# At most two loads to a place, and a conversion load only where there is no other: the order of SP's transfers in an attention and feed-forward kernel

## The chip, the cores and the metric

The kernel runs on one core of a Trainium2 chip. The metric is the device time of one execution in microseconds. The profile shows one execution, with its own times counted from the start of its span.

## The reference

Attention with its heads mixed before and after the softmax, then a feed-forward layer with the gate h - tanh(h). Batch 8, 12 heads, 448 rows, head dimension 64; 3584 tokens of 768, inner dimension 2048.

```python
scores = scale * np.matmul(q, k.transpose(0, 1, 3, 2))
scores = np.einsum('bhij,hg->bgij', scores, w_pre)
attn = softmax(scores)                      # over the last axis
attn = np.einsum('bhij,hg->bgij', attn, w_post)
x = np.matmul(attn, v)                      # then heads side by side: 3584 x 768
h = x @ w_in
out = (h - np.tanh(h)) @ w_out
```

In the kernel, `w_in` and `w_out` arrive as 64-bit numbers; they are turned on the chip into pairs of 32-bit parts (high and low) and written back to DRAM, from where the feed-forward stage reads them.

## The kernel before, in words

**Places.** Attention is cut into 32 blocks (8 batches of 4 runs of up to 120 rows), and these into 360 groups of rows. The main loop (L832) goes through places p = 0 to 182; places up to 179 take two groups each. A place issues, in this order: the gathers of the groups two places ahead (L507, tile `t` from the scores `s`), up to six waiting transfers (`issue`, L372), the mix of heads before the softmax (`premix`, L513, into `ps_p`), the normalizer of the place before (`norm`, L536: DVE's `zs`, POOL's `wr` at L543), the softmax (`expo`, L524: DVE's maxima at L530, ACT's exponentials at L532), then scores, preparation of q and k, and values by a table of places, then the mix after the softmax of the place before (`mix`, L548: PE at L560 into `ps_o`). The copy of `ps_o` to `at` on ACT (L570, L577) is issued at the start of the next place.

**The queues.** All these gathers and transfers are issued by SP, in the order of the program. Loads of q, k and v and stores of the result x go to a Python list `queue`; those of the conversion of weights go to a second list, `slow`. `issue(6)` sends up to six entries at each place: first from `queue`, then from `slow`, each list in its own order, and only what was asked for in an earlier place. `now` (L635) sends all that waits.

**The conversion.** `narrow_steps` (L38) goes through 56 chunks of the weights. Up to three chunks are loaded or at work, up to two at work. A chunk is taken up when its load was sent in an earlier place (`landed(1)`). `narrow_chunk` (L71) does one in eleven steps: DVE L80, ACT L82 with DVE L83, ACT L85, DVE L87, DVE L89, DVE L94, POOL L96, POOL L98, ACT L102, POOL L104, and the request of two stores. Tiles: `cr` the load, `cm`, `cs`, `cl` buffers, two of each; `ws` the place in DRAM. `Steps.place` (L861, in every place from 4 on) runs steps at a fixed rate, 617 steps over 164 places; a step taken while no chunk is at work does nothing. At place 177 `conv.rest(now)` (L867) runs all that is left, sending each transfer at once.

**The end of attention.** After that, still in place 177, SP issues the first weight tile (`w`, L334) and twelve loads of x (`rx`, L238). Place 178 casts the first x on ACT (`xh`, L246), place 180 the other five, and place 181 runs the first hidden matmuls of the feed-forward stage (L257 to L262).

Of the kernel before, what the change touches and what calls it, by code (L numbers as in the profile page):

```python
# [18 lines left out]
DRAM = bass.MemoryType.DRAM  # L19
# [129 lines left out]
def kernel_body(  # L149
# [189 lines left out]
    with ExitStack() as st:  # L339
# [20 lines left out]
        queue, slow, sent = [], [], {}  # L360
# [6 lines left out]
        def send(x, engine):  # L367
            entry = x.pop(0)
            engine.dma_start(*entry[1:3])
            entry[3] = place[0]  # L370

        def issue(most):  # L372
            for x in (queue, slow):
                while x and most and x[0][0] < place[0]:
                    send(x, nc.sync)
                    most -= 1

# [306 lines left out]
        for w in range(2):  # L684
            for at in AT[w]:
                x = repeat[:, w, at : at + HP].rearrange("p (i h) -> p i h", i=GH)
# [7 lines left out]
        for w in range(2):  # L694
            for a in range(2):
                if w == 0:
                    x = both[:, w, a].rearrange("p (i g) -> p i g", i=GH)
                    of, step = ps_w[:, w, :].unsqueeze(1).to_broadcast([P, GH, H]), [[H, GH], [0, H]]
                else:
                    x = both[:, w, a].rearrange("p (g i) -> p g i", i=GH)  # L700
# [68 lines left out]
        while halved:  # L769
            ready = sorted((x for x in halved if x[0] <= p), key=lambda x: (x[1], x[3:]))  # L770
            if ready:
                x = ready[0]
# [3 lines left out]
                if x[2] == kind and other and x[1] > p + 1:  # L776
                    x = other[0]
# [54 lines left out]
        for p in range(NPL + 3):  # L832
# [4 lines left out]
            for t in (2 * p + 4, 2 * p + 5):  # L837
                if t < NG:
                    gather(t)
            issue(6)  # L840
            if p == NPL + 1:
                for f in start.pop(p):
# [105 lines left out]
```

## Time and profile before

| | |
|---|---|
| median of 3 runs | 1788.36 us |
| lowest and highest | 1786.55 and 1803.96 us |
| the profiled execution's own time | 1788.92 us |
| its span | 1787.2 us |
| mean granted clock of TensorE | 0.993 |
| transfers issued by SP: gathers `t` | 342 of 210 KB, 16 of 189 KB |
| loads of the conversion `cr` | 24 of 512 KB, 32 of 384 KB |
| stores of the conversion `ws` | 48 of 256 KB, 64 of 192 KB |
| loads of v, k, q | 24 and 23 of 448 KB, 23 of 360 KB and 8 of 264 KB |

Attention lasts until about 845 us of the span; there the first hidden matmul starts. In the rows of a timeline, the first number is the start in us, the second the length, then engine, line, operation, tiles and count; in brackets stands how long the engine had been idle and what released it. `SPq` is the queue of SP, and its rows are the issues of transfers, not the transfers.

### The profile page before, as it was taken

Reading aid. Unit: us, or ns where it says so; the run is one execution under the profiler, and the core shown is the slowest. Engines: PE = TensorE matmul, PEld = TensorE weight load, DVE = VectorE, ACT = ScalarE, POOL = GpSimd, SP = SyncE. Lnnn points to the kernel's source line nnn. Section 1 sums busy time; section 2 is a strip of 40 time slices with the busy share of each in tenths; the row PEclk is TensorE's granted clock in tenths of the full one; section 3 lists DMA queues with packets and bytes.
Section 4 is the critical chain, followed back from the end, with each engine's and each line's share of the span. In section 5 each row is a group of like instructions: output and inputs, shape, how many; then the busy total and the mean of one; then the engine's idle time right before and its main releaser. Section 6 shows DMA issues by size and latency. Waiting matters only on the chain.

```text
span 1787.2 us, 41382 instructions
## 1 busy us (share of the span) xinstructions
PE 1751.0 (98%) x16572; PEld 1425.6 (80%) x16572; DVE 1128.3 (63%) x2362; ACT 1000.5 (56%) x2051; POOL 320.1 (18%) x417
## 2 busy tenths in 40 slices
PE   8999999999999999999999999999999999999998
PEld 6777777777777777777888888888888888888887
DVE  5676777777777767664556566565565565655555
ACT  5777877777777776765343443433434434444333
POOL 1333333333333333321010010000000000000000
PEclk9999999999999999999999999999999999999999
DMA  8668687777967687565655655655656655655651
GB/s 176 204 196 216 194 236 224 217 215 215 249 203 218 215 213 220 178 202 216 255 207 194 248 193 207 241 193 214 229 197 216 224 208 204 228 217 190 230 194 36
DMA packets 232816, 372.32 MB, mean 208 GB/s; under 512 B 98992, under 2 KB 207536, under 8 KB 218288
## 3 DMA queue, kind: packets, MB, share of 16 engines
q1 hardware_dynamic: 231740, 368.45, 64.0%
q8 instruction: 131, 2.15, 0.5%
q10 hardware_dynamic: 884, 1.22, 0.2%
q14 instruction: 61, 0.50, 0.1%
HBM read 245.37 MB, written 47.19 MB: 164 GB/s over the span
## 4 chain that ended last, share of the span: by engine, by line
PE 87%; DMA 4%; ACT 4%; DVE 3%; issue 1%; POOL 0%; SPq 0%; ACTq 0%; DVEq 0%; POOLq 0%
PE ps_o L560 13%; PE ps_h L257 8%; PE ps_h L258 8%; PE ps_h L262 8%; PE ps_m L602 8%; PE ps_p L521 7%; PE ya L305 6%; PE ya L302 6%; PE ya L303 6%; PE ps_q L477 5%; PE yb L305 3%; PE yb L303 3%; PE yb L302 3%; DMA t<-s 2%; PE ps_m L443 1%
## 5 line engine op out<-in xcount | busy, mean ns | idle before, releaser
L560 PEld LDWEIGHTS ps_o<-wr,e 60*112 60x112 f32 (+1 forms) x5760 | 306.2, 176 | 44.3 <-POOL wr L543 21.8
L560 PE MATMUL ps_o<-wr,e 60*112 60x60 f32 (+1 forms) x5760 | 315.5, 259 | 14.3 <-POOL wr L543 7.7
L530 DVE TENSOR_REDUCE mx<-ps_p 128x1 f32<-128x448 f32 x360 | 207.7, 619 | 163.9 <-PE ps_p L521 163.7
L532 ACT ACTIVATE e<-ps_p,mx 128x448 f32<-128x448 f32 x360 | 225.7, 634 | 101.9 <-DVE mx L530 99.4
L289 ACT CAST gh<-r 128x512 fp32r<-128x512 f32 x112 | 69.6, 621 | 372.6 <-DVE r L282 372.6
L258 PE MATMUL ps_h<-xl,w 128*128 128x512 f32 x672 | 264.4, 393 | 0.0
L257 PE MATMUL ps_h<-xh,w 128*128 128x512 f32 x672 | 264.3, 393 | 0.0
L570 ACT COPY at<-ps_o 112x960 f32<-112x960 f32 x156 | 153.7, 985 | 93.8 <-PE ps_o L560 93.2
L247 POOL TENSOR_TENSOR xl<-rx,xh 128x512 fp32r<-128x512 f32 x38 | 55.6, 1464 | 731.2 <-ACT xh L246 731.2
L521 PE MATMUL ps_p<-t,wpre 60*64 60x448 f32 (+1 forms) x1440 | 180.8, 569 | 3.9 <-DMA t<-s 2.7
L305 PE MATMUL ya<-w,gl 128*128 128x512 f32 x448 | 177.0, 395 | 0.7 <-DVE gl L290 0.7
L278 DVE SCALAR_TENSOR_TENSOR r<-qa,ps_h 128x512 f32<-128x512 f32 x112 | 77.1, 688 | 159.2 <-ACT t L275 159.2
L302 PE MATMUL ya<-w,gh 128*128 128x512 f32 x448 | 174.8, 390 | 1.0 <-ACT gh L289 1.0
L303 PE MATMUL ya<-w,gh 128*128 128x512 f32 x448 | 174.8, 390 | 0.0
L602 PEld LDWEIGHTS ps_m<-at,vr 112*64 112x64 f32 x3072 | 147.5, 137 | 31.0 <-ACT at L577 10.9
L262 PE MATMUL ps_h<-xh,w 128*128 128x512 f32 x672 | 170.6, 389 | 0.0
L602 PE MATMUL ps_m<-at,vr 112*64 112x120 f32 (+1 forms) x3072 | 161.6, 261 | 8.4 <-ACT at L577 3.1
L272 ACT ACTIVATE u<-ps_h 128x512 f32<-128x512 f32 x112 | 67.0, 599 | 152.9 <-PE ps_h L262 152.9
L262 PEld LDWEIGHTS ps_h<-xh,w 128*128 128x128 f32 x672 | 126.3, 188 | 26.3
L258 PEld LDWEIGHTS ps_h<-xl,w 128*128 128x128 f32 x672 | 127.5, 190 | 23.7
L257 PEld LDWEIGHTS ps_h<-xh,w 128*128 128x128 f32 x672 | 127.4, 190 | 23.4
L543 POOL TENSOR_TENSOR wr<-wpost,zs 128x120 f32<-128x120 f32 x180 | 70.2, 390 | 402.9 <-DVE zs L542 293.6
(93 smaller groups left out, 3038.0 us busy)
## 6 DMA issues: line engine op xcount, KB each, us to landing
w<-ws SPq DMA_DIRECT2D x112, 1536.0 KB
t<-s SPq DMA_DIRECT2D x342, 210.0 KB
cr<-in_moe_w_in_dram SPq DMA_DIRECT2D x24, 512.0 KB
cr<-in_moe_w_out_dram SPq DMA_DIRECT2D x32, 384.0 KB
vr<-in_v_dram SPq DMA_DIRECT2D x24, 448.0 KB
kr<-in_k_dram SPq DMA_DIRECT2D x23, 448.0 KB
out_dram<-ob SPq DMA_DIRECT2D x24, 384.0 KB
qr<-in_q_dram SPq DMA_DIRECT2D x23, 360.0 KB
```

What stands on the lines that cost most here:

```text
L257: nc.tensor.matmul(ph, wh[:, fs], xh, start=(c == 0), stop=False)
L258: nc.tensor.matmul(ph, wh[:, fs], xl, start=False, stop=False)
L262: nc.tensor.matmul(ph, wl[:, fs], xh, start=False, stop=(c == NK - 1))
L302: nc.tensor.matmul(y, gh[:, tok], wh[:, es], start=first, stop=False)
L303: nc.tensor.matmul(y, gh[:, tok], wl[:, es], start=False, stop=False)
L305: nc.tensor.matmul(y, gl[:, tok], wh[:, es], start=False, stop=last)
L521: nc.tensor.matmul(pss[r][halves[j], :], wpre[k, :], ts[j][k, :], start=True, stop=True)
L530: nc.vector.tensor_reduce(out=mx, in_=ps, axis=AX.X, op=ALU.max, negate=True)
L532: nc.scalar.activation(e, ps, AF.Exp, bias=mx, scale=1.0, accum_out=zs[:, 0, r : r + 1])
L560: nc.tensor.matmul(ps[:CP, j, c * GP : (c + 1) * GP].rearrange("p (h i) -> p h i", i=GI)[:, :, r * GH : (r + 1) * GH], e[k, c * CP : (c + ...
L570: nc.scalar.copy(ats[i0][:, :, :, at : at + 2 * GI].rearrange("p c h (j i) -> p j (c h) i", j=2), ps[:CP, :, : NC * GP].rearrange("p j (x ...
L602: nc.tensor.matmul(pv[j * D : (j + 1) * D, r, :n], vt[:, j, c, :], ats[i][:, c, 2 * hp + j, :n], start=(c == 0), stop=(c == NC - 1),)
```

## The change

`issue` counts the loads that it sends at a place (entries whose target is not in DRAM). It stops with a list when two loads have gone, and stops with `slow` at a load if any load has gone at that place. Stores are not counted, but one that stands behind a held load in its list waits with it.

```diff
         def issue(most):
+
+            loads = 0
             for x in (queue, slow):
                 while x and most and x[0][0] < place[0]:
+                    if x[0][1].space != DRAM:
+                        if loads == 2 or loads and x is slow:
+                            break
+                        loads += 1
                     send(x, nc.sync)
                     most -= 1
```

From L375 on, lines of the changed kernel stand six lower (L510 is L516 there). Every engine has as many instructions as before; their order moves. On SP, at places 4 to 8, where the conversion begins (`kr`, `qr` loads of k and q, `cr` loads of the conversion, `t` gathers; two gathers are one place), before:

```order
L369 DMA kr<-in_k_dram 112x16x64
L510 DMA t<-s 120x1x448 x2
L369 DMA qr<-in_q_dram 88x12x64
L369 DMA cr<-in_moe_w_in_dram 128x1024 x3
L510 DMA t<-s 120x1x448 x8
```

and now:

```order
L369 DMA kr<-in_k_dram 112x16x64
L516 DMA t<-s 120x1x448 x2
L369 DMA qr<-in_q_dram 88x12x64
L516 DMA t<-s 120x1x448 x2
L369 DMA cr<-in_moe_w_in_dram 128x1024
L516 DMA t<-s 120x1x448 x2
L369 DMA cr<-in_moe_w_in_dram 128x1024
L516 DMA t<-s 120x1x448 x2
L369 DMA cr<-in_moe_w_in_dram 128x1024
```

The three loads that stood in one place behind the load of q stand in the three places after it.

On SP at place 177, behind the last gathers (`ws` stores of the conversion, `w` the first weight tile, `rx` the first x), before:

```order
L510 DMA t_110<-s_12367 108x1x448
L510 DMA t_111<-s_12367 108x1x448
L334 DMA w0_12920<-ws0_65 128x3072
L238 DMA rx_12922<-xs0_57 128x448
L238 DMA rx_12922<-xs1_58 128x64
```

and now:

```order
L516 DMA t_110<-s_12295 108x1x448
L516 DMA t_111<-s_12295 108x1x448
L369 DMA ws3_68<-cs_12588 128x384
L369 DMA ws3_68<-cl_12758 128x384
L369 DMA ws3_68<-cs_12753 128x384
L369 DMA ws3_68<-cl_12883 128x384
L369 DMA ws3_68<-cs_12876 128x384
L369 DMA ws3_68<-cl_12894 128x384
L334 DMA w0_12920<-ws0_65 128x3072
L238 DMA rx_12922<-xs0_57 128x448
L238 DMA rx_12922<-xs1_58 128x64
```

The stores of the last three chunks, which went out some places earlier, stand between the last gathers and the loads of the next stage.

On POOL, from place 176 to place 178 (`wr` of `norm`; `cm`, `cl` of the conversion), before:

```order
L543 TENSOR_TENSOR wr_12799<-wpost_186,zs_12764 128x2x60
L543 TENSOR_TENSOR wr_12841<-wpost_186,zs_12804 128x2x60
L215 MEMSET bias_12917 128x1
L216 MEMSET bias_12917 128x1
L543 TENSOR_TENSOR wr_12947<-wpost_186,zs_12846 128x2x60
```

and now:

```order
L549 TENSOR_TENSOR wr_12814<-wpost_186,zs_12774 128x2x60
L96 TENSOR_TENSOR cm_12752<-cr_12521,cs_12753 128x384
L98 TENSOR_TENSOR cm_12752<-cm_12752,cr_12521 128x384
L104 TENSOR_TENSOR cl_12883<-cm_12752,cs_12753 128x384
L96 TENSOR_TENSOR cm_12875<-cr_12707,cs_12876 128x384
L98 TENSOR_TENSOR cm_12875<-cm_12875,cr_12707 128x384
L104 TENSOR_TENSOR cl_12894<-cm_12875,cs_12876 128x384
L215 MEMSET bias_12917 128x1
L216 MEMSET bias_12917 128x1
L549 TENSOR_TENSOR wr_12947<-wpost_186,zs_12819 128x2x60
```

The last two chunks' POOL steps stand between the `wr` of place 177 and that of place 178. On ACT, two steps L102, one L82 and one L85 stand in the same way ahead of the copy of `ps_o` that begins place 178.

## The prediction

> **What bounds the kernel now.** I read the page's first part for the engines, then the stretches (busy time by engine over windows that I chose), then the chain of work that ended last in order of time.
>
> ```profile
> span 1787.2 us, 41382 instructions
> PE 1751.0 (98%) x16572; PEld 1425.6 (80%) x16572; DVE 1128.3 (63%) x2362; ACT 1000.5 (56%) x2051; POOL 320.1 (18%) x417
> ```
>
> PE is idle for 36 us of the whole span, so no change that leaves its matmuls alone can win more than that and the stretches in which its clock is cut. The change touches attention only. The second view has, for each stretch, PE, PEld, DVE, ACT and POOL busy, the granted clock, the DMA share and GB/s:
>
> ```profile
> 30.00:790.00 760.00, 737.98 (x10876) 572.15 (x10868) 542.83 (x1466) 571.00 (x1302) 250.03 (x333) 0.99 0.74 214
> 42.00:57.00 15.00, 12.75 (x186) 9.93 (x184) 9.87 (x28) 11.39 (x27) 1.55 (x4) 1.00 0.90 256
> 158.00:176.00 18.00, 15.29 (x238) 12.13 (x234) 10.15 (x29) 11.65 (x30) 5.36 (x8) 1.00 0.91 230
> 560.00:592.00 32.00, 29.97 (x435) 22.84 (x435) 22.92 (x62) 23.67 (x55) 10.06 (x15) 1.00 0.84 228
> 662.00:676.00 14.00, 12.60 (x182) 9.56 (x180) 7.80 (x21) 8.19 (x17) 5.03 (x6) 1.00 1.02 268
> ```
>
> From 30 to 790 us PE idles 22.0 us. The four short stretches are the ones where the chain (start, length, what) runs through a long transfer:
>
> ```profile
> 45.49 7.76 DMA cr<-in_moe_w_in_dram
> 160.36 6.53 DMA t<-s
> 563.26 7.96 DMA t<-s
> 571.23 8.19 DMA cr<-in_moe_w_out_dram
> 663.77 7.87 DMA vr<-in_v_dram
> ```
>
> PE's idle time there is 2.25 + 2.71 + 2.03 + 1.40 = 8.4 us. That is all that a better spacing of loads can be seen to be worth; the other 13.6 us stand at places where ACT and DVE are late with score copies, maxima and conversion steps, of which the change removes none.
>
> **The change part by part.** It adds and removes no instruction: every engine issues the same number before and now (848 on SP, 2180 on DVE). It moves loads to later places, and with them the conversion steps, which need a load of an earlier place.
>
> **The first loads.** Three weight loads and a q load went out in one place; now each has its own. What that cost:
>
> ```profile
> 43.96 2.46 SPq L369 DMA_DIRECT2D cr<-in_moe_w_in_dram  x3
> 51.86 0.43 DVE L80 TENSOR_SCALAR cm<-cr 128x512 f32<-128x512 f32 x1 [0.90 <-DMA cr<-in_moe_w_in_dram]
> 55.28 2.68 PE L602 MATMUL ps_m<-at,vr 112*64 112x120 f32 x48 [1.82 <-ACT at L570]
> ```
>
> The first load landed 7.9 us after its issue began; L80 held up DVE, and at the end of that queue PE stood for 1.82 us. I count 2.0 of that stretch's 2.25 us as won. The other three stretches (6.1 us) are the pile of k, v and q loads at a change of batch, which now keeps conversion loads out, but still has q and v together: half, 3.0 us. Gain 5.0 us, between 0 and 8.4.
>
> **What it gives back on DVE.** A conversion load now goes out late and is used as soon as it may be. Counted in the order of instructions, L80 follows its load by one place in 27 of 56 chunks (11 before), and L87, which writes the buffer that the store of the chunk two earlier reads, follows that store by one place or less in 29 (18 before). DVE works in order, so a transfer that is late there holds up the maxima behind it (L530), for which ACT's exponentials wait. Before, that cost DVE:
>
> ```profile
> DVE cm L80 <- DMA cr<-in_moe_w_in_dram: 3.4, 4, 1.0
> DVE cs L87 <- DMA ws<-cs: 6.9, 3, 3.5
> ```
>
> 10.3 us in 29 such cases, 0.36 us each. 27 more at that price are 9.6 us; at nothing, if a load that is alone in its place lands in time, 0. I take 1.5 us: of the 3.4 us the first three loads made 1.9, and they are spread now.
>
> **The end of the conversion.** Conversion steps come at a fixed rate, and a step with no landed chunk is lost. Before, all chunks were done some places early; now the last two are unfinished at place 177, where `conv.rest` does what is left in one go. All engines issue in order, so everything of places 178 and 179 queues behind it. Before, that place ran so:
>
> ```profile
> 827.28 0.49 SPq L334 DMA_DIRECT2D w<-ws  x1
> 828.78 1.16 DVE L530 TENSOR_REDUCE mx<-ps_p 128x1 f32<-128x448 f32 x2 [0.70 <-PE ps_p L521]
> 829.42 8.07 SPq L238 DMA_DIRECT2D rx<-xs  x12
> 831.38 0.79 DVE L620 COPY x<-ps_m 128x360 f32<-128x360 f32 x1 [1.45 <-PE ps_m L602]
> 832.59 0.39 POOL L543 TENSOR_TENSOR wr<-wpost,zs 128x120 f32<-128x120 f32 x1 [3.88 <-DVE zs L542]
> 833.09 0.98 ACT L570 COPY at<-ps_o 112x960 f32<-112x960 f32 x1 [2.23 <-PE ps_o L560]
> 836.00 0.61 ACT L246 CAST xh<-rx 128x512 fp32r<-128x512 f32 x1
> 836.50 1.78 PE L560 MATMUL ps_o<-wr,e 60*112 60x60 f32 x32
> 838.33 0.98 ACT L570 COPY at<-ps_o 112x960 f32<-112x960 f32 x1 [1.72 <-PE ps_o L560]
> 839.46 1.78 PE L560 MATMUL ps_o<-wr,e 60*112 60x60 f32 x32 [0.26 <-ACT at L570]
> 842.40 2.42 PE L560 MATMUL ps_o<-wr,e 60*112 60x60 f32 x32 [1.16 <-POOL wr L543]
> ```
>
> And one chunk's steps, from the last chunk of before:
>
> ```profile
> 782.69 0.35 DVE L80 TENSOR_SCALAR cm<-cr 128x384 f32<-128x384 f32 x1
> 782.96 0.36 DVE L83 TENSOR_SCALAR cr<-cr 128x384 int32<-128x384 int32 x1
> 792.37 0.35 DVE L87 TENSOR_SCALAR cs<-cr 128x384 int32<-128x384 int32 x1
> 792.75 0.56 DVE L89 SCALAR_TENSOR_TENSOR cr<-cm,cs 128x384 int32<-128x384 int32 x1
> 793.35 0.36 DVE L94 TENSOR_SCALAR cs<-cr 128x384 int32<-128x384 int32 x1
> 793.84 1.01 POOL L96 TENSOR_TENSOR cm<-cr,cs 128x384 f32<-128x384 f32 x1 [4.70 <-ACT s L482]
> 795.16 1.02 POOL L98 TENSOR_TENSOR cm<-cm,cr 128x384 f32<-128x384 f32 x1
> 796.21 0.51 ACT L102 CAST cs<-cm 128x384 fp32r<-128x384 f32 x1
> 796.80 0.99 POOL L104 TENSOR_TENSOR cl<-cm,cs 128x384 fp32r<-128x384 f32 x1 [0.62 <-ACT cs L102]
> ```
>
> Put on the times of before: the maxima end at 829.9; L89 and L94 of the last chunk but one follow until 830.9. POOL: L96 and L98 until 833.0; ACT's L102 until 833.6; L104 until 834.7. The last chunk's five DVE steps (2.0 us after L620, until 834.2) lie beside that. Then L96 and L98 until 836.7, L102 until 837.3, L104 until 838.4, with about 0.1 us at each change of engine. Behind it on ACT stands the copy of `ps_o` (L570): 837.4 instead of 833.09. Behind it on POOL stands `wr` (L543): 838.5 instead of 832.59. The mix on PE that needs both starts at 839.0 instead of 836.50, since the values before it cover the rest: 2.5 us lost.
>
> SP is the worse queue. The last store waits for L104, and the first weight tile and the twelve loads of x stand behind it: 838.5 instead of 827.28 for w, and 839.0 instead of 829.42 for the first x. The cast that reads it (L246) stands on ACT in place 178, ahead of the next copy of `ps_o`. In the trace of before x had landed by 836.00, at most 8.7 us after w was issued; so now L246 starts at 847.2 at the latest, and at 839.8 at the earliest, after its own place's exponentials. I take 845, nearer the late end, because w's 1.5 MB go out ahead of it on the same queue. Then the next copy of `ps_o` starts at 845.6 instead of 838.33, the mix at 839.46 and all behind it go back by 7.3 us, up to the first hidden matmul. This holds the 2.5 us within it: the term is 7.3 us, between 2.5 and 9.5.
>
> **The clock.** After a gap PE also runs slower for a while:
>
> ```profile
> 795.26 3.00 PE L560 MATMUL ps_o<-wr,e 60*112 60x60 f32 x32 [1.26 <-POOL wr L543]
> 790.00:800.00 10.00, 8.74 (x98) 6.02 (x96) 5.32 (x15) 6.27 (x14) 3.67 (x5) 0.78 0.35 127
> 840.00:850.00 10.00, 8.84 (x70) 7.50 (x68) 2.79 (x7) 5.82 (x12) 3.11 (x4) 0.67 0.68 283
> ```
>
> The clock was 0.78 around a gap of 1.26 us (2.2 us lost in 10) and 0.67 in the ten microseconds that the drain now hits (3.3 us). A longer gap there adds between nothing and another 3.3 us; I take 1.5. The Trainium skill (TensorE: Matmul & The Clock Gate, section "What's actually happening") lets the clock fall to half only after an idle window of about 3.4 us. The row of 795.26 speaks against it, with a cut clock at a gap of 1.26 us; by the rule the gap of some five microseconds before 845.6 would be charged and the first one not, so the estimate would hardly move.
>
> **The sum**, against the profiled execution's own 1788.92 us (span 1787.2 and 1.7 around it; the median of the runs is 1788.36, 0.6 less): 1788.9 - 5.0 + 1.5 + 7.3 + 1.5 = 1794.2, so 1794 us.
>
> **The rivals.** First: the end hides, and the spacing pays in full. x would land as soon as ACT reaches its cast; for it speaks that ACT had idled 1.72 us before the next copy, against it that SP issues x ten microseconds later. 1788.9 - 8.4 + 2.5 = 1783.0. Second, slower: DVE's own waits. If loads and stores one place old are as late as before, every further case costs the 0.36 us, and DVE has no room (543 of 760 us busy, and PE reaches its maxima in every place); with no gain from spacing, 1788.9 + 9.6 + 8.8 = 1807.3. It decides from 0.31 us a case on: 27 of them make 8.5 us, which with the end's 8.8 is 1%. Against it: each load has its place to itself. Third: the spacing does not do what it says, because the same bytes pass in the same 180 places and the gathers are held by k and v anyway; the end remains: 1788.9 + 8.8 = 1797.7.
>
> **How the numbers follow.** The forecast has 0.5, the first rival 0.2, the third 0.2, the second 0.1. A range from 1784 to 1805 holds the forecast, the third, most of the bounds of the end, and all but the tip of the others. About 1%, 17.9 us, is what a measurement of this kernel can tell from no change: below 1770.5 lies no case (0.02 for what I overlooked), above 1806.2 only the second rival with a full price (0.06), and 0.92 is left between.
>
> **What would show it.** Right: L80's wait at 51 us gone; PE idle in 30 to 790 us down by 2 to 6 us; POOL's L96, L98, L104 twice in a row just ahead of the first load of w; `xh` (L246) waiting for `rx` for some microseconds; the first hidden matmul, which followed the mix that ended at 844.8, about 4 to 6 us later (gain and loss together); everything after it as before. Wrong: x's loads issued as early as before, DVE waits on L80 and L87 well above 12 us in all, or a changed length of the stage behind the first hidden matmul.

## The result, and the profile after

| | before | after |
|---|---|---|
| median of 20 runs each, on the same chip | 1789.01 us | 1802.07 us |
| ratio | | 1.006, 95% interval 1.0047 to 1.0073 |
| the profiled execution's own time | 1788.92 us | 1800.04 us |
| its span | 1787.2 us | 1798.3 us |
| mean granted clock of TensorE | 0.993 | 0.988 |

The change makes the kernel 0.6% slower (the two medians lie 13.1 us apart). That is within 1%, as forecast, and inside the range, but 8 us above the predicted 1794. The profiled execution is 11.1 us longer, and I follow these 11.1 us.

First the stretches of the prediction (busy time of PE, PEld, DVE, ACT and POOL, granted clock, DMA share, GB/s), in the changed kernel:

```profile
30.00:790.00 760.00, 740.60 (x10882) 575.52 (x10880) 530.85 (x1448) 567.72 (x1291) 238.74 (x321) 0.99 0.73 209
42.00:57.00 15.00, 14.57 (x226) 11.61 (x226) 9.07 (x26) 11.85 (x28) 1.16 (x3) 1.00 0.85 216
158.00:176.00 18.00, 18.00 (x268) 13.99 (x262) 11.38 (x34) 11.05 (x26) 2.02 (x5) 1.00 0.91 265
560.00:592.00 32.00, 31.72 (x468) 24.48 (x470) 22.07 (x63) 24.20 (x59) 7.69 (x12) 1.00 0.87 238
662.00:676.00 14.00, 14.00 (x204) 10.98 (x200) 8.22 (x22) 10.09 (x23) 4.88 (x6) 1.00 0.91 267
```

In the four short stretches PE's idle time fell from 8.4 us to 0.7 (79 less 14.57, 18.00, 31.72 and 14.00). From 30 to 790 us it fell only from 22.0 to 19.4. So outside the four it rose from 13.6 to 18.7. The first row shows something else: DVE has 12.0 us less work behind it at 790 us (530.85 after 542.83) and POOL 11.3 us less (238.74 after 250.03). The conversion is that far behind.

The end of the conversion in the changed kernel, as a timeline from place 177 to the first hidden matmul:

```profile
824.78 1.16 DVE L536 TENSOR_REDUCE mx<-ps_p 128x1 f32<-128x448 f32 x2 [1.03 <-PE ps_p L527]
828.04 1.19 POOL L98 TENSOR_TENSOR cm<-cm,cr 128x384 f32<-128x384 f32 x1
828.27 1.17 DVE L83 TENSOR_SCALAR cr<-cr 128x384 int32<-128x384 int32 x1
829.84 1.39 POOL L104 TENSOR_TENSOR cl<-cm,cs 128x384 fp32r<-128x384 f32 x1 [0.62 <-ACT cs L102]
830.41 1.04 DVE L94 TENSOR_SCALAR cs<-cr 128x384 int32<-128x384 int32 x1
834.14 0.97 ACT L576 COPY at<-ps_o 112x960 f32<-112x960 f32 x1
834.31 1.00 POOL L104 TENSOR_TENSOR cl<-cm,cs 128x384 fp32r<-128x384 f32 x1 [0.62 <-ACT cs L102]
835.71 0.42 SPq L334 DMA_DIRECT2D w<-ws  x1
836.18 8.56 SPq L238 DMA_DIRECT2D rx<-xs  x12
836.83 2.43 PE L566 MATMUL ps_o<-wr,e 60*112 60x60 f32 x32 [4.27 <-POOL wr L549]
843.25 0.62 ACT L246 CAST xh<-rx 128x512 fp32r<-128x512 f32 x1 [6.90 <-DMA rx<-xs]
843.77 0.97 ACT L576 COPY at<-ps_o 112x960 f32<-112x960 f32 x1
845.50 3.25 PE L566 MATMUL ps_o<-wr,e 60*112 60x60 f32 x32 [4.53 <-POOL wr L549]
849.91 3.25 PE L566 MATMUL ps_o<-wr,e 60*112 60x60 f32 x32 [1.17 <-ACT at L576]
853.09 0.79 PE L257 MATMUL ps_h<-xh,w 128*128 128x512 f32 x1
```

Before, the maxima of place 177 began at 828.78 (quoted in the prediction), and the first hidden matmul as follows:

```profile
844.75 0.79 PE L257 MATMUL ps_h<-xh,w 128*128 128x512 f32 x1
```

DVE's first wait for a conversion load, at 51.86 before, in the changed kernel:

```profile
54.66 0.43 DVE L80 TENSOR_SCALAR cm<-cr 128x512 f32<-128x512 f32 x1 [1.93 <-DMA cr<-in_moe_w_in_dram]
```

Three marks cut the span: the maxima of place 177, the first hidden matmul, the end.

| | to place 177 | from there to the first hidden matmul ("the end") | behind it | span |
|---|---|---|---|---|
| before | 828.8 | 16.0 | 942.4 | 1787.2 |
| after | 824.8 | 28.3 | 945.2 | 1798.3 |
| difference | -4.0 | +12.3 | +2.8 | +11.1 |

The loss is in the 28 us at the end. Whether the 4.0 us ahead of it are a gain, or work that was put off, the next section asks.

### The profile page after: what moved, and what is told of

It reads as the page before. It is cut to its first block, busy times and chain, and to the rows that moved or that the text cites. A ratio compares the mean times of both kernels' runs of the same rounds, so it can differ in the third digit from the quotient of the medians.

```text
span 1798.3 us, 41370 instructions
## 1 busy us (share of the span) xinstructions
PE 1753.8 (98%) x16572; PEld 1428.7 (79%) x16572; DVE 1125.6 (63%) x2362; ACT 1001.4 (56%) x2051; POOL 320.6 (18%) x417
## 4 chain that ended last, share of the span: by engine, by line
PE 87%; ACT 4%; DVE 3%; DMA 2%; issue 2%; POOL 1%; SPq 0%; ACTq 0%; DVEq 0%; POOLq 0%
PE ps_o L566 13%; PE ps_h L257 8%; PE ps_h L258 8%; PE ps_h L262 8%; PE ps_m L608 8%; PE ps_p L527 7%; PE ya L305 6%; PE ya L302 6%; PE ya L303 6%; PE ps_q L483 6%; PE yb L305 3%; PE yb L303 3%; PE yb L302 3%; DVE mx L536 1%; PE ps_m L449 1%
## 5 line engine op out<-in xcount | busy, mean ns | idle before, releaser
L608 PEld LDWEIGHTS ps_m<-at,vr 112*64 112x64 f32 x3072 | 149.2, 138 | 28.2 <-ACT at L583 11.5
L277 DVE TENSOR_SCALAR far<-u 128x512 f32<-128x512 f32 x112 | 47.8, 427 | 145.4 <-ACT u L272 137.0
```

The costliest lines, as they stand in the source:

```text
L608: nc.tensor.matmul(pv[j * D : (j + 1) * D, r, :n], vt[:, j, c, :], ats[i][:, c, 2 * hp + j, :n], start=(c == 0), stop=(c == NC - 1),)
```

## The experiments

The columns of this table are those above, of each profiled execution; ratios are those to the kernel before, which ran beside them at medians of 1791.92 us (first four rows), 1791.19 (next four) and 1792.73 (last four), so that kernels are compared by their ratios. Edits are to the changed kernel unless the text says otherwise.

| | place 177 | end | behind | median us | ratio, 95% interval |
|---|---|---|---|---|---|
| all steps done before place 177 | 828.2 | 16.7 | 942.3 | 1790.21 | 0.999 (0.9973 to 1.0006) |
| before, slower rate | 826.9 | 28.2 | 940.7 | 1802.05 | 1.0055 (1.0037 to 1.0073) |
| cap of two alone | 829.3 | 15.7 | 941.7 | 1787.99 | 0.9975 (0.9957 to 0.9993) |
| conversion alone in its place | 828.6 | 28.4 | 943.3 | 1804.86 | 1.005 (1.0028 to 1.0073) |
| first cast of x later | 829.4 | 24.0 | 943.5 | 1800.30 | 1.0052 (1.0032 to 1.0073) |
| last stores behind w and x | 826.7 | 22.4 | 949.0 | 1803.19 | 1.0066 (1.0045 to 1.0086) |
| conversion loads also beside one other | 839.6 | 16.2 | 942.5 | 1799.92 | 1.0048 (1.003 to 1.0067) |
| PE kept busy in the gaps | 825.6 | 27.3 | 941.8 | 1800.34 | 1.0051 (1.0032 to 1.007) |
| one chunk left instead of two | 823.7 | 26.5 | 945.4 | 1799.50 | 1.0039 (1.0021 to 1.0056) |
| last stores behind, with filler | 837.2 | 23.5 | 947.5 | 1804.55 | 1.0064 (1.0038 to 1.0089) |
| cap of two alone, again | 827.0 | 16.4 | 942.4 | 1788.96 | 0.9981 (0.9965 to 0.9997) |
| cap of two, faster rate | 830.9 | 16.8 | 941.3 | 1790.28 | 0.9988 (0.9968 to 1.0009) |

**The spacing without the end.** The two rules stay; the steps run fast enough to be done by place 173.

```diff
-        conv = Steps(..., 11 * len(chunks) + 1, NPL - 16)
+        conv = Steps(..., 11 * len(chunks) + 1, NPL - 32)
```

> The changed kernel with the conversion's steps run faster (617 steps over 148 places instead of 164), so that all 56 chunks are done by place 173 and nothing is left for place 177. Theory (the loss is the left-over conversion at place 177; the spacing itself won the 4.0 us by which place 177 was reached earlier): the 12.4 us of the end and the 2.7 us behind it go, the 4.0 us stay: 1789.0 - 4.0 = 1785, 0.998 of before, first hidden matmul at about 841 us. Rival one (the 4.0 us were only the work of two chunks put off to the end): 1789, 1.000 of before, first hidden matmul at about 845. Rival two (the spacing itself costs, the end is a symptom): 1795 or more, place 177 later than 829.

The first stretch, and the end, of this kernel:

```profile
30.00:790.00 760.00, 740.97 (x10842) 573.99 (x10834) 535.99 (x1459) 569.30 (x1297) 245.84 (x328) 0.99 0.74 212
```

```profile
826.71 0.48 SPq L334 DMA_DIRECT2D w<-ws  x1
828.22 1.15 DVE L536 TENSOR_REDUCE mx<-ps_p 128x1 f32<-128x448 f32 x2 [0.70 <-PE ps_p L527]
835.45 0.61 ACT L246 CAST xh<-rx 128x512 fp32r<-128x512 f32 x1
```

The w load is issued ahead of the maxima again, as before, the cast of x waits for nothing, and the end is 16.7 us. The loss is gone. So is nearly all of the lead, as the first rival had it: place 177 comes 0.6 us earlier than before, not 4.0. PE's idle time from 30 to 790 us is still 3.0 us below that of before (19.0 us), and still no gain arrives: the span is 1787.2 us, that of before to the tenth. Most of the 4.0 us were therefore conversion steps that had not been run yet. (One part of the missing gain is the clock, as the section on the prediction shows.)

**The end without the spacing.** The kernel before, its loads untouched, with a rate that leaves steps for place 177. SP's order from place 174 on is that of the change, and so is POOL's from place 176 on.

```diff
-        conv = Steps(..., 11 * len(chunks) + 1, NPL - 16)
+        conv = Steps(..., 11 * len(chunks) + 1, NPL - 4)
```

> The kernel before, loads as they were, with the steps run slower (617 over 176 places), so that its POOL and SP order at places 174 to 177 is the same as the changed kernel's: two chunks left for place 177. Theory: the end alone costs what it cost in the change, 12.4 us up to the first hidden matmul and up to 2.7 behind it; if putting off two chunks wins nothing before it: 1789 + 15 = 1804, 1.008; if putting off wins 4.0 us: 1800, 1.006. Rival (spacing is the cause): 1790 or less, within 0.2% of before.

Its end (line numbers of the kernel before):

```profile
826.94 1.15 DVE L530 TENSOR_REDUCE mx<-ps_p 128x1 f32<-128x448 f32 x2 [0.70 <-PE ps_p L521]
837.55 0.42 SPq L334 DMA_DIRECT2D w<-ws  x1
845.33 0.62 ACT L246 CAST xh<-rx 128x512 fp32r<-128x512 f32 x1 [7.14 <-DMA rx<-xs]
847.58 3.25 PE L560 MATMUL ps_o<-wr,e 60*112 60x60 f32 x32 [3.97 <-POOL wr L543]
```

The same end (28.2 us) and the same time as the change; it lies between my two cases, 1800 and 1804. With the experiment before, this shows that the end is enough for the loss, and needed for it.

**The two halves of the rule.** One kernel keeps only the cap of two loads to a place, the other only the rule that a conversion load goes alone.

```diff
-                        if loads == 2 or loads and x is slow:
+                        if loads == 2:
```

> Half the rule: at most two loads to a place, a conversion load may be one of them. The conversion ends at place 170 as before. Theory: no end, and the part of the spacing gain that the first three loads and the k, v, q piles bring: 1786 to 1788, 0.998 to 0.9995. Rival (the cap holds back what the next places need): 1792 or more.

```diff
-                        if loads == 2 or loads and x is slow:
+                        if loads and x is slow:
```

> The other half: a conversion load goes out only where no other load does; no cap of two on the others. The order on POOL at places 176 and 177 is that of the change. Theory: all of the loss is here: 1800 to 1803, 1.006 to 1.008. Rival (the cap of two is what costs): 1790 or less.

The cap alone sends its last store at place 170, as before, and has none of the loss: 0.9975. The other half gives 1.005, with an end of 28.4 us. So the loss is all in the words "and one of the conversion only where there is no other".

**Which waits make up the end.** Three kernels take one of them away each. The first moves the cast of x that stood ahead of the copy of `ps_o`:

```diff
-            NPL - 2: x0[:1],
+            NPL - 2: [],
...
-                for f in x0[1:]:
+                for f in x0:
```

> The changed kernel, but the first cast of x (ACT, place 178) is put with the other five at place 180, so that no copy of ps_o stands behind it on ACT. Of the 12.3 us that the end costs from the maxima of place 177 to the first hidden matmul, theory one (ACT stands behind a late x, 6.9 us of waiting) says the mix of place 179 comes some 5 us earlier, but the hidden matmuls still need all of x, which lands at about 847 to 850: 2 to 4 us won, 1798 to 1800. Theory two (the POOL and ACT steps of the conversion are the whole of it): nothing won, 1802.

The second lets w and x go out ahead of the last two chunks' stores; for this the conversion's buffers must outlive the stage, and tiles of the next stage move:

```diff
+        cv = ctx.enter_context(tc.tile_pool(name="cv", bufs=1, side="left"))
         ld = early.enter_context(...)
         sp = early.enter_context(...)
-        cv = early.enter_context(tc.tile_pool(name="cv", bufs=1, side="left"))
...
-                conv.rest(now)
+                now()
+                conv.rest(lambda: None)
```

(`gpool` is opened in `open_late` instead of `open_early`.)

> The changed kernel, but the stores of the last two chunks go out behind the first weight tile and x on SP (two pools keep their memory longer for that). The conversion steps at place 177 stay as they are on DVE, ACT and POOL. Theory one (x is late because SP stands at the stores): x lands before ACT reaches its cast, the wait of 6.9 us is gone, and only the 4.3 us by which the mix of place 178 is late, with some clock, remain: 7 to 9 us of the 13 won, 1793 to 1795. Theory two (POOL and ACT steps are the whole of it): nothing won, 1802.

The third runs matmuls that nobody reads ahead of the mixes of places 178 and 179, so that PE stands still for less time there. Each call of `busy` gives 36 instructions on PE in the trace, 4.29 us long together:

```diff
+            if p in {NPL - 2: 18, NPL - 1: 18}:
+                busy({NPL - 2: 18, NPL - 1: 18}[p], ps_m.tile([P, 512], F32, name="ps_b", tag="ps_m"))
             if 1 <= p < NPL + 1:
                 mixed = mix(p - 1)
```

> The changed kernel with 18 small matmuls, whose result nobody reads, ahead of each of the two mixes that wait at places 178 and 179 (3.8 us each at full clock, in gaps of 4.3 and 4.5 us). They change nothing that is waited for. If the cut clock there follows from PE's idle time, the two mixes take 1.8 us instead of 3.25 and the hidden matmuls run at full speed: 3 to 5 us won, 1797 to 1799. If the clock is cut for another reason, or the waits hide it: 1802.

The mixes of the last one:

```profile
837.63 1.78 PE L566 MATMUL ps_o<-wr,e 60*112 60x60 f32 x32
846.71 1.78 PE L566 MATMUL ps_o<-wr,e 60*112 60x60 f32 x32 [2.17 <-POOL wr L549]
849.66 3.25 PE L566 MATMUL ps_o<-wr,e 60*112 60x60 f32 x32 [1.17 <-ACT at L576]
```

The end shrinks by 4.3 us without the early cast, by 5.9 with w and x ahead of the stores, by 1.0 with PE busy. The two mixes take 1.78 us instead of 2.43 and 3.25, that is 2.1 us less, of which 1.0 reaches the end; after the next gap, of 1.17 us, the third is slow again. In the times none of the three can be told from the change: their intervals all hold 1.006, where I had expected 2 to 4, 7 to 9 and 3 to 5 us. So these three ends are readings of one profiled execution each. The second also paid for its gain behind the end: its stage there is 949.0 us long.

**Tiles that moved.** To find out why, the same kernel with a filler, meant to let `gpool` begin at a multiple of 128 bytes again:

```diff
     def open_late():
+        fill = ctx.enter_context(tc.tile_pool(name="fill", bufs=1, side="left"))
+        nc.gpsimd.memset(fill.tile([P, LINE - 2], F32, name="fill", tag="fill"), 0.0)
         ff.gp = ctx.enter_context(...)
```

> The order of the experiment with the last stores behind w and x, but with a filler of 120 bytes ahead of the feed-forward stage's pool, so that its tiles begin at a multiple of 128 bytes again. Theory (tiles that begin 8 bytes off made its matmuls 394 instead of 391 ns): the feed-forward stage's matmuls are back at 389 to 391 ns, the stage from the first hidden matmul to the end at 942 to 945 us instead of 949.0, the end at 22 to 23 us, and the time 1795 to 1799 us. Rival (the matmuls are slower because all tiles of the stage stand further up, or because two stores pass beside them): 394 ns again and 1802 us or more.

The hidden matmuls with `xh` from 860 us on (busy us, mean ns): first the change, then the kernel with the last stores behind w and x, then the one with the filler.

```profile
L257 PE MATMUL ps_h<-xh,w 128*128 128x512 f32 x666 | 260.4, 391 | 0.0
```

```profile
L258 PE MATMUL ps_h<-xh,w 128*128 128x512 f32 x664 | 261.7, 394 | 0.0
```

```profile
L260 PE MATMUL ps_h<-xh,w 128*128 128x512 f32 x672 | 263.9, 393 | 0.0
```

The matmuls with `xl` give 391, 393 and 392 ns in the same order. The filler does not bring the matmuls back to 391 ns, and the stage is still 947.5 us long. My theory of the 8 bytes fails; what makes them slower (all tiles stand further up here, by the size of the conversion's pool, and two stores pass in the first microseconds) stays open. The end is 23.5 us, so the order on SP is again worth some 5 us of the end, and the time is again no better than the change's.

**How the loss grows with what is left.** Steps a little faster: one chunk's last steps are left at place 177, not two chunks'.

```diff
-        conv = Steps(..., 11 * len(chunks) + 1, NPL - 16)
+        conv = Steps(..., 11 * len(chunks) + 1, NPL - 24)
```

> The changed kernel with the conversion's rate set for 24 places before the end instead of 16: the last conversion load goes out at place 173 instead of 175, the store of the last chunk but one follows place 176, and only one chunk's last three steps and its two stores are left at place 177. Theory (the drain at place 177 holds w and x by what it has left to do, step by step): the end, 28.3 us in the change and 16.0 before, comes to between 21 and 25 us, and the time to 1795 to 1799 us. Rival (any drain costs all of it, since w stands behind a store in any case and x behind w): the end stays over 26 us and the time at 1799 us or more. Rival (the last chunk alone hides beside the queue of maxima and mixes): end below 19 us, time as before.

Its end:

```profile
823.67 1.15 DVE L536 TENSOR_REDUCE mx<-ps_p 128x1 f32<-128x448 f32 x2 [0.70 <-PE ps_p L527]
827.96 0.36 DVE L94 TENSOR_SCALAR cs<-cr 128x384 int32<-128x384 int32 x1
831.18 1.00 POOL L104 TENSOR_TENSOR cl<-cm,cs 128x384 fp32r<-128x384 f32 x1 [0.62 <-ACT cs L102]
832.58 0.42 SPq L334 DMA_DIRECT2D w<-ws  x1
840.36 0.62 ACT L246 CAST xh<-rx 128x512 fp32r<-128x512 f32 x1 [7.14 <-DMA rx<-xs]
```

I had expected 21 to 25 us; the end is 26.5, and the first rival's bound (over 26) holds. Half the work that is left costs 10.5 of the 12.3 us. The place explains it: with two chunks left w is issued 10.9 us after the maxima of place 177 begin (835.71), with one left 8.9 us (832.58), and before it went out 1.5 us ahead of them (827.28). The first of the two chunks runs beside the maxima and copies of its place and makes w 2 us later. The last one begins behind them, and then its five engine changes, its store and the loads follow one after the other. Where stores stand ahead of w, the end follows the issue of w: against the maxima of place 177, w goes out 10.4 us later than before with one chunk left, 12.1 in the kernel before at the slower rate and 12.4 in the change, and the ends are 10.5, 12.2 and 12.3 us longer. With this one point between nothing and two chunks, the loss looks like a step and not like a slope: one chunk left is nearly everything lost. What a few steps of the last chunk would cost was not measured.

**The slower rival's mechanism.** A cap that lets conversion loads go beside exactly one other load.

```diff
-                        if loads == 2 or loads and x is slow:
+                        if loads == 2:
                             break
-                        loads += 1
+                        loads += 1 if x is queue else 2
```

> A rule between the two: at most two loads to a place, at most one of them of the conversion, which may go beside one other. The conversion ends at place 170 as before. If the spacing is worth something once the end is left alone: 1785 to 1787, 0.998; if the idle time that it takes away at the piles of loads comes back at other places, as in the first run of the faster steps: 1789, within 0.2% of before.

The edit is looser than that text: beside one other load it sets no limit to the conversion's loads. On SP this matters once, in the first place of the conversion, where again three of them stand behind one load of q. Elsewhere 19 conversion loads have one other load in their place and 34 have none; under the cap of two alone it is 19 with one other, 35 with none and two together.

DVE's waits for the conversion's transfers in that kernel (total, times, longest), and the longest with the load that it waited for and what followed:

```profile
DVE cm L80 <- DMA cr<-in_moe_w_out_dram: 10.2, 2, 7.3
DVE cs L87 <- DMA ws<-cs: 7.5, 3, 5.7
DVE cm L80 <- DMA cr<-in_moe_w_in_dram: 6.1, 4, 2.7
```

```profile
361.70 1.17 SPq L369 DMA_DIRECT2D cr<-in_moe_w_out_dram  x1
371.79 0.36 DVE L80 TENSOR_SCALAR cm<-cr 128x384 f32<-128x384 f32 x1 [7.34 <-DMA cr<-in_moe_w_out_dram]
372.89 1.10 PE L483 MATMUL ps_q<-kk,qh 64*120 64x448 f32 x3 [3.00 <-DVE zs L547]
```

The conversion ends in time and the end is 16.2 us, but place 177 comes 10.8 us late, and the time is 1.0048 of before; neither of the two cases came. DVE waits 23.8 us for these transfers. One load, sent right behind a load of v in its place and used at the next, is 7.34 us late and holds up PE for 3.00 us. From 30 us to place 177 PE idles 26.7 us, 3.2 more than before, and the trace's record of the clock has it at half for 25.2 us instead of 14.6, which is some 5.3 us of work; 10.2 of the 25.2 begin at that stall. The other 2 us stay open. So the rival's mechanism exists; in the change itself it did not occur, as the next section shows. But the cap of two has nearly the same loads side by side and is not slower. Which load meets which place differs between the two, and no run here separates that from the rule.

**The better half again, and with a faster rate.** The cap of two alone once more, with twelve runs as the first time, and with `NPL - 24` beside it.

> The half of the change that caps loads at two to a place, alone, again and in more rounds, since it was 0.9975 of the time before with an interval that ended at 0.9993. If the half gains, about 0.997 to 0.999 again, 1784 to 1787 us; if that was chance, 1.000.

> The cap of two alone with the rate set for 24 places before the end: the conversion ends at place 161 instead of 169, and conversion loads stand alone in 38 places instead of 35. If the gain of the cap comes from spacing, this has at least as much, 0.996 to 0.999; if DVE's waits for loads one place old eat it (17 cases of L80 and 25 of L87 instead of 13 and 20), 1.000 or more.

Again faster, 0.9981, its interval again just below 1: twice 0.2 to 0.25%, some 4 us. With the faster rate 0.9988, which cannot be told from either 1 or the cap alone, though DVE then waits far more for one kind of load than the 3.4 us of before:

```profile
DVE cm L80 <- DMA cr<-in_moe_w_in_dram: 14.0, 6, 3.8
```

With its other two waits (6.3 and 4.4) it waits 24.7 us in all, more than the 23.8 of the kernel above, and yet it is not slower; the sum of DVE's waits alone does not set the time. The best kernel of the study is the cap of two without the second rule. Why it gains is not shown: with the faster rate more conversion loads stand alone (38 places instead of 35), and no larger gain can be seen.

## Why the prediction was right or wrong

The forecast of "within 1%" and the range hold. The time is 8 us above the number, and of the four cases the third rival (the spacing does nothing, only the end counts, 1797.7) came closer than the forecast. Step by step:

**The gain of the spacing, -5.0: this step failed.** The stalls in the four stretches did go (7.7 of 8.4 us), more than the 5.0 I counted. (The four are not all: the chain also ran through long transfers at 269, 303, 348 and 362 us. PE idled 1.0 us in those stretches, which my 8.4 left out.) But I took idle time of PE that goes in one place for time that the kernel wins: 5.1 us came back in other places. One of them, behind a conversion step that now ran there, in the changed kernel:

```profile
255.64 0.62 ACT L102 CAST cs<-cm 128x512 fp32r<-128x512 f32 x1 [2.46 <-POOL cm L98]
256.16 0.97 ACT L576 COPY at<-ps_o 112x960 f32<-112x960 f32 x1
257.18 4.34 PE L608 MATMUL ps_m<-at,vr 112*64 112x120 f32 x48 [2.22 <-ACT at L576]
```

ACT stood 2.46 us for POOL's step, the copy behind it was late, and PE stood for 2.22 us. The stretch from 230 to 270 us had no idle time before. The first load's wait did not vanish either: it went from 51.86 to 54.66 us and from 0.90 to 1.93 us, only PE no longer felt it. The rest of what seems won, the lead of 4.0 us at place 177, is work put off, as the kernel with all its steps done shows (0.6 us). By its time, 0.999 of before with an interval from -4.8 to +1.1 us, a net gain of 3.5 us as I had summed it would still be possible; but the kernel with the end alone costs as much as the change (1.0055 and 1.006), which speaks against any such gain. In the profiled execution with all steps done PE idles 3.0 us less up to 790 us, and 2.7 less up to place 177, and 0.6 us arrives there. Some 1.2 us of the difference is the clock: from 30 us to place 177 the trace's record has it at half for 17.1 us in that kernel and for 14.6 before. The rest stays open. I had weighed how late the piled loads were, but not that the rule moves the 27 conversion loads that had shared a place (29 of 56 had one to themselves before), and their steps with them, to other places, of which the one shown had had no idle time.

**DVE's give-back, +1.5: too much.** DVE's waits for these transfers were 11.9 us before: the prediction's 10.3 left out a third row, the first one here. They fell to 3.8 in the changed kernel, the other two:

```profile
DVE cm L80 <- DMA cr<-in_moe_w_out_dram: 1.6, 2, 1.2
DVE cm L80 <- DMA cr<-in_moe_w_out_dram: 1.9, 3, 1.0
DVE cm L80 <- DMA cr<-in_moe_w_in_dram: 1.9, 1, 1.9
```

Of the 56 loads, each alone in its place, DVE waits for four, at most 1.9 us. The bound at nothing was right, and the second rival (1807.3) is out for this kernel. One place of lead can be too little when loads stand together, as the load of 361.70 in the kernel that lets them go beside one other showed.

**The end, +7.3 and +1.5 for the clock: right in mechanism, too small.** Every link is there: POOL's two chains ahead of the load of w, the copy of `ps_o` late (9.4 us after the maxima instead of 4.3; I had 8.6), the stores ahead of w on SP, the cast of x waiting 6.90 us, the copy behind it late. Taken against the maxima of place 177, that second copy starts at 19.0 us, where it was at 9.55: 9.4 us later, at the upper bound of 2.5 to 9.5. Two durations made the difference to 7.3. w went out 10.9 us after the maxima, where I had 9.7: DVE and POOL ran slowly while they worked at the same time: L83 took 1.17 us, L94 1.04 and L104 1.39 in the rows above, 0.36, 0.36 and 0.99 in the rows that I had used. And x landed 7.5 us after w was issued (835.71 to 843.25), where my 845 stood for 6.5 behind 838.5. Then 0.6 us for `wr`, which waits for DVE's part of the cast, and 2.3 us by which the last two mixes are slower (3.25 us each, where they took 1.78 and 2.42). That makes 12.3; the prediction had 8.8. In the kernel with PE kept busy 1.0 us of such loss was won back at the end.

**The rest, which was to stay as before:** it is 2.8 us longer in the profiled execution of the change. Some 1.7 of these are the clock, which goes to half once more behind a stretch (890 to 895 us) in which PE stood for 1.5 us:

```profile
895.00:900.00 5.00, 4.89 (x18) 4.03 (x19) 3.81 (x7) 1.41 (x3) 0.00 (x0) 0.66 0.01 2
```

In the kernels with an end of over 26 us the stage measured 945.2 and 945.4 us where there was such a cut, and 940.7, 943.3 and 941.8 us where there was none, so it is no steady part of the loss.

In sum: no gain where I had 3.5 us net, and 12.3 where I had 8.8, both wrong in the same direction, are 7.0 of the 8 us. Three rows of "what would show it" were missed: L80's first wait is not gone, the first hidden matmul is 8.3 us later than before, not 4 to 6, and the stage behind it changed its length, which was one of my signs of being wrong. PE's idle time down by 2.6 us fell inside its bounds without meaning what I took it to mean.

## What to carry to other kernels

Before counting idle time that goes as a gain, ask what work has moved out of that stretch, and when it will be due: here a fixed-rate background job was spread better and finished later, and its tail stood in front of the next stage's first loads on an in-order queue. The price of such a tail need not shrink with it: half of it cost 10.5 of the 12.3 us. So look at the last item of a background job first, and try a rule's halves apart: here the cap alone was 0.2% faster, and the rule that holds conversion loads back 0.5% slower.

## What the runs showed of the hardware

The granted clock stayed at half for far longer than the gaps. Windows of the changed kernel (columns as above):

```profile
845.00:850.00 5.00, 3.34 (x34) 3.19 (x34) 1.44 (x5) 2.55 (x6) 0.77 (x2) 0.50 0.95 311
850.00:855.00 5.00, 5.00 (x37) 4.50 (x38) 1.89 (x3) 3.34 (x7) 2.72 (x3) 0.50 0.89 372
855.00:860.00 5.00, 5.00 (x19) 3.74 (x19) 0.00 (x0) 0.09 (x1) 0.00 (x0) 0.67 0.04 17
```

PE is busy without a break from 849.91 us on, and the clock is at 0.50 until 855 and at 0.67 in the five microseconds behind. The mean of 0.67 over the last five, at two levels of half and full, puts the change at 858.3 us, 8.4 us after the break ended. The Trainium skill (TensorE: Matmul & The Clock Gate, section "What's actually happening") has the full clock come back after at least one busy window of about 3.4 us, and lets the windows run free of the kernel; in this trace 8.4 us passed, more than two such windows.

Short gaps were enough to cut it. From 30 us to place 177 every stretch at half clock in the profiled executions of before and of the change begins within 2.3 us of the end of a gap of PE of 1.0 to 2.2 us, and no gap there is longer than that. Not every such gap has a cut behind it: the one of 1.82 us before the row of 55.28 in the prediction has none.

In the profiled execution of the kernel with the filler a gap of 1.04 us is followed by 14 us at a clock of 0.52:

```profile
372.84 0.63 PE L569 MATMUL ps_o<-wr,e 60*112 60x60 f32 x2 [1.04 <-issue]
373.00:387.00 14.00, 14.00 (x110) 10.45 (x112) 5.43 (x14) 7.00 (x16) 0.39 (x1) 0.52 0.81 247
```

The kernel without the filler has as much idle time of PE from 350 to 390 us (busy 38.67 of 40 us in both) at full clock. Up to place 177 the clock was at half for 35.7 us with the filler and for 13.7 without, and half of that difference, 11.0 us, is about what place 177 came later (10.5). Why one gap cuts the clock and another does not stays open. This is why I trust a few microseconds of one profiled execution less than the ratios.

In the change's row of 828.27, L83 on DVE, 0.36 us long in the prediction's rows, lasts until 829.44, and POOL's L98 beside it until 829.23; L94 lasts until 831.45 and POOL's L104 until 831.23. Both DVE steps end 0.2 us behind the POOL step that had begun ahead of them. The Trainium skill (SBUF — State Buffer, section "SBUF: two separate sides") says that GpSimd and a DVE operation in a two-port mode exclude each other for a whole instruction; the four rows agree with that, and no run here tested it by itself. In a drain that runs two chunks at once, one chunk's DVE steps and the other's POOL steps so cost more than each alone.

Matmuls became 2 to 3 ns longer (391 to 393 and 394 ns) when the tiles of their stage were placed elsewhere, in the two kernels whose stage behind the end was 949.0 and 947.5 us long, after 942.4 before and 945.2 in the change.
